# SBUF homes of a fused attention and feed-forward kernel: all operands of the 128x512 matmuls at one remainder modulo 512 bytes

## The chip, the cores and the metric

The kernel runs on one core of a Trainium2 chip. The metric is the time of one execution on the device in microseconds (us); a single execution of it is also recorded by the hardware profiler, which gives a start and an end for nearly every instruction. SBUF is the on-chip memory that the engines read their operands from; an address here is the byte offset of a tile within each of the 128 partitions.

## The reference

The inputs are q, k and v of shape (4, 8, 768, 64) in float32 and two weights in float64, `w_in` (512 x 2048) and `w_out` (2048 x 512). Attention is local (window of 16) with a summary key and value for each block of 32 positions, and its output is the input of a feed-forward layer:

```python
k_sum = k.reshape(B, H, nb, block, D).max(axis=3)
v_sum = v.reshape(B, H, nb, block, D).mean(axis=3)
scores_l = scale * np.matmul(q, k.transpose(0, 1, 3, 2))          # |i - j| < 16 is kept
scores_s = scale * np.einsum('bhsd,bhnd->bhsn', q, k_sum) + np.log(block)
a = softmax(concatenate([scores_l_masked, scores_s], axis=-1))
x = np.matmul(a, concatenate([v, v_sum], axis=2))                 # to (3072, 512)
h = x @ w_in
g = h * np.tanh(softplus(h))
return (g @ w_out).astype(np.float32)
```

## The kernel before

**The feed-forward part.** The 3072 tokens are worked in 6 groups `g` of 512, and the 2048 hidden units in 16 blocks `fc` of 128, so there are 96 steps `(g, fc)`. Every factor is held as two tiles, an upper and a lower part (`hi`/`lo`, `xh`/`xl`, `ah`/`al`), and each product is made of three matmuls. `ff_in` (L421) makes the hidden block `ph` with 12 matmuls (L427): four slices `cc` of `w_in` as the stationary operand, `xh` and `xl` as the moving one, 512 columns each. `ff_act` (L434) takes it out of PSUM, `ff_split` (L443, L445) makes `ah` and `al` of it. `ff_out` (L447) adds to four output tiles `po` with 12 matmuls (L455): four slices of `ah` or `al` are stationary, `w_out` moves, 512 columns each. One step is thus two groups of 12 matmuls of 128x512, a `ph` group and a `po` group, and there are 96 x 24 = 2304 such matmuls. In each group the three of a triple come in the order upper times upper, upper with the other's lower part, lower.

**Weights.** The weights arrive as 64-bit words and are split on ScalarE and VectorE into `hi` and `lo` during the first part of the run. Blocks `fc` 0 to 9 lie in the tiles `w_early_in`, `w_early_out`, blocks 10 to 15 in `w_late_in`, `w_late_out`. The late tiles take over the room of the pools `first_att` and `first_more` (L165, L166), which serve the first attention units and are closed at L587.

**Attention.** Each unit is a chunk of 256 positions and a pair of heads: scores `sc` (L317, for the first units L321 and L323), exponents and their sums on ScalarE and VectorE (L339, L350), normalizing on GpSimd (L370), four transposes `pt_ps` (L376), values `x_ps` (L397, L403), and the split into `xh` and `xl` (L413, L414). Units of the next token group stand between the `ph` and `po` groups of the present one.

**Order.** The order of the instructions is written out by hand: a list of short words (L546) for the first steps, where `ph`, `po` and the weight work are mixed, and after it a loop in which step `i` issues `ff_in` of step `i`, the attention work that falls due, and `ff_out` of step `i - 2` (L635). So in the loop `ph` and `po` groups alternate. Nothing reorders it (`tc.manual_schedule()`, L581).

**Homes.** A pool is opened on one of two sides of SBUF, and tiles get addresses in the order in which the pools are opened: `left` upwards, `right` downwards from the top. The pools are opened at L65 to L71.

Of the kernel before, what the change touches and what calls it, by code (L numbers as in the profile page):

```python
# [9 lines left out]
F32 = mybir.dt.float32  # L10
# [10 lines left out]
P = 128  # L21
# [18 lines left out]
EARLY = 10  # L40
# [17 lines left out]
def fused_kernel(ctx: ExitStack, tc: tile.TileContext, q0, qk, kt, v0, vw, vs, w_in, w_out, out):  # L58
# [3 lines left out]
    def pool(name, bufs, side):  # L62
        return ctx.enter_context(tc.tile_pool(name=name, bufs=bufs, side=side))

    const = pool("const", 1, "left")  # L65
    xp = pool("xp", 2, "left")
    w_out_home = pool("w_out_home", 1, "right")
    ff = pool("ff", 3, "right")
    stage = pool("stage", 2, "left")
    small = pool("small", 8, "right")  # L70
    att = pool("att", 2, "right")  # L71
    ps_o = ctx.enter_context(tc.tile_pool(name="ps_o", bufs=4, space=PS))

    ps_w = ctx.enter_context(tc.tile_pool(name="ps_w", bufs=4, space=PS))
# [27 lines left out]
    def weight_tiles(pools, name, blocks):  # L102
        return [[home.tile([P, blocks, WP], F32R, name=f"{name}_{w}_{part}") for part in ("hi", "lo")]
                for w, home in zip(("in", "out"), pools)]

    early = weight_tiles((const, w_out_home), "w_early", EARLY)
    late = []

    def weight(w, part, fc):
# [460 lines left out]
    def parse(word):  # L570
        name = next(m for m in sorted(ops, key=len, reverse=True) if word.startswith(m))
        return name, word[len(name):]
# [10 lines left out]
    for k, word in enumerate(order):  # L583
        name, what = parse(word)
# [101 lines left out]
```

## Time and profile before

| | |
|---|---|
| runs | 642.46, 643.26, 644.35 us (median 643.26) |
| the profiled execution | 643.47 us, of which the span from the first to the last instruction is 641.8 us |
| busy: TensorE matmul / weight load | 625.0 us / 510.3 us |
| busy: VectorE / ScalarE / GpSimd | 288.8 us / 270.3 us / 74.8 us |
| TensorE clock granted, mean over the span | 0.997 of full speed |

How to read it: the ends of matmuls in the trace are modelled and overlap the next matmul, so the mean duration of a matmul is not its cost. What a matmul costs is the time from its start to the start of the next one, called its *pitch* below. The timeline gives starts to 0.01 us; the pitch of one matmul is therefore read over several.

### The profile page before, as it was taken

Reading aid. Unit: us, or ns where it says so; the run is one execution under the profiler, and the core shown is the slowest. Engines: PE = TensorE matmul, PEld = TensorE weight load, DVE = VectorE, ACT = ScalarE, POOL = GpSimd, SP = SyncE. Lnnn points to the kernel's source line nnn. Section 1 sums busy time; section 2 is a strip of 40 time slices with the busy share of each in tenths; the row PEclk is TensorE's granted clock in tenths of the full one; section 3 lists DMA queues with packets and bytes.
Section 4 is the critical chain, followed back from the end, with each engine's and each line's share of the span. In section 5 each row is a group of like instructions: output and inputs, shape, how many; then the busy total and the mean of one; then the engine's idle time right before and its main releaser. Section 6 shows DMA issues by size and latency. Waiting matters only on the chain.

```text
span 641.8 us, 10991 instructions
## 1 busy us (share of the span) xinstructions
PE 625.0 (97%) x4272; PEld 510.3 (80%) x4272; DVE 288.8 (45%) x817; ACT 270.3 (42%) x659; POOL 74.8 (12%) x119
## 2 busy tenths in 40 slices
PE   4899899999999999999999999999999999999997
PEld 4787788777888888888888888888888888888885
DVE  4999999984232435323223445423232232222221
ACT  4986668582433425414425434245244251111111
POOL 4421131120101001001001011010010010000000
PEclk9999899999999999999999999999999999999999
DMA  9977765642212234603203254333133010100001
GB/s 285 280 243 261 229 228 191 209 161 96 64 46 76 84 112 115 215 1 96 83 14 95 91 150 131 90 91 95 66 95 86 11 32 1 65 1 0 1 0 66
DMA packets 31780, 68.24 MB, mean 106 GB/s; under 512 B 6768, under 2 KB 11632, under 8 KB 31728
## 3 DMA queue, kind: packets, MB, share of 16 engines
q1 hardware_dynamic: 31728, 67.53, 33.7%
q8 instruction: 34, 0.56, 0.4%
q14 instruction: 18, 0.15, 0.1%
HBM read 59.11 MB, written 6.29 MB: 102 GB/s over the span
## 4 chain that ended last, share of the span: by engine, by line
PE 90%; DVE 5%; DMA 1%; issue 1%; ACT 1%; POOL 1%; SPq 0%; POOLq 0%
PE po L455 41%; PE ph L427 39%; PE x_ps L403 3%; PE pt_ps L376 3%; PE sc L317 3%; DVE pr L339 1%; DMA q<-q 1%; DVE w_f L153 1%; DMA vw<-vm 1%; POOL pr L370 1%; DVE w L140 1%; PE sc L321 0%; DVE w_f L148 0%; DVE km L244 0%; DVE w L144 0%
## 5 line engine op out<-in xcount | busy, mean ns | idle before, releaser
L434 ACT ACTIVATE a<-ph 128x512 f32<-128x512 f32 x96 | 57.3, 598 | 249.1 <-PE ph L427 165.5
L443 DVE CAST ah<-a 128x512 fp32r<-128x512 f32 x80 | 34.1, 426 | 237.3 <-ACT a L434 235.9
L370 POOL TENSOR_TENSOR pr<-pr,rs 128x480 f32<-128x480 f32 x48 | 54.9, 1144 | 360.7 <-DVE rs L366 211.3
L455 PE MATMUL po<-w_early_out_hi,ah 128*128 128x512 f32 x240 | 96.0, 400 | 0.0
L427 PE MATMUL ph<-xh,w_early_in_hi 128*128 128x512 f32 x240 | 95.3, 397 | 0.0
L455 PE MATMUL po<-w_early_out_hi,al 128*128 128x512 f32 x240 | 94.5, 394 | 0.1
L427 PE MATMUL ph<-xh,w_early_in_lo 128*128 128x512 f32 x240 | 94.2, 392 | 0.0
L455 PE MATMUL po<-w_early_out_lo,ah 128*128 128x512 f32 x240 | 94.0, 392 | 0.0
L427 PE MATMUL ph<-xl,w_early_in_hi 128*128 128x512 f32 x240 | 93.4, 389 | 0.0
L350 ACT ACTIVATE pr<-pr,nm 128x120 f32<-128x120 f32 x192 | 73.3, 384 | 8.9 <-DVE nm L339 8.7
L445 DVE TENSOR_TENSOR al<-a,ah 128x512 fp32r<-128x512 f32 x96 | 68.7, 716 | 3.4 <-ACT ah L443 0.7
L455 PE MATMUL po<-w_late_out_hi,ah 128*128 128x512 f32 x144 | 57.5, 400 | 0.0
L427 PE MATMUL ph<-xh,w_late_in_hi 128*128 128x512 f32 x144 | 57.5, 399 | 0.0
L455 PE MATMUL po<-w_late_out_hi,al 128*128 128x512 f32 x144 | 56.8, 395 | 0.0
L455 PE MATMUL po<-w_late_out_lo,ah 128*128 128x512 f32 x144 | 56.7, 394 | 0.0
L427 PE MATMUL ph<-xh,w_late_in_lo 128*128 128x512 f32 x144 | 56.6, 393 | 0.0
L427 PE MATMUL ph<-xl,w_late_in_hi 128*128 128x512 f32 x144 | 56.1, 389 | 0.0
L455 PEld LDWEIGHTS po<-w_early_out_hi,ah 128*128 128x128 f32 x240 | 45.5, 189 | 11.3 <-issue 1.9
L427 PEld LDWEIGHTS ph<-xh,w_early_in_lo 128*128 128x128 f32 x240 | 45.0, 188 | 10.5
L455 PEld LDWEIGHTS po<-w_early_out_lo,ah 128*128 128x128 f32 x240 | 45.4, 189 | 9.8
L455 PEld LDWEIGHTS po<-w_early_out_hi,al 128*128 128x128 f32 x240 | 45.5, 190 | 9.6 <-DVE al L445 0.6
L427 PEld LDWEIGHTS ph<-xl,w_early_in_hi 128*128 128x128 f32 x240 | 45.2, 188 | 9.7
(77 smaller groups left out, 825.4 us busy)
## 6 DMA issues: line engine op xcount, KB each, us to landing
qk<-qk SPq DMA_DIRECT2D x40, 496.0 KB
w<-w_in SPq DMA_DIRECT2D x16, 512.0 KB
w<-w_out SPq DMA_DIRECT2D x16, 512.0 KB
vw<-vw SPq DMA_DIRECT2D x40, 192.0 KB
ks<-kt SPq DMA_DIRECT2D x16, 384.0 KB
out<-o SPq DMA_DIRECT2D x24, 256.0 KB
vsum<-vs SPq DMA_DIRECT2D x12, 384.0 KB
vw<-vm SPq DMA_DIRECT2D x40, 48.0 KB
```

The source lines that it names most:

```text
L140: nc.vector.tensor_scalar(out=x, in0=x, scalar1=29, scalar2=None, op0=ALU.logical_shift_right)
L153: nc.vector.scalar_tensor_tensor(out=u, in0=u, scalar=3, in1=words(k)[0], op0=ALU.logical_shift_left, op1=ALU.bitwise_or)
L317: nc.tensor.matmul(ps[h][row, at0:at0 + KA], u["qk"][r, s, h * QT:(h + 1) * QT], u["qk"][r, s, P:], start=True, stop=True)
L350: nc.scalar.activation(pr[:, s, :], pr[:, s, :], AF.Exp, scale=-1.0, bias=nm[:, s:s + 1], accum_out=sm[:, s:s + 1])
L370: nc.gpsimd.tensor_mul(u["p"], u["p"], u["r"].unsqueeze(2).broadcast_to([P, NQ, KA]))
L376: nc.tensor.transpose(ps[:KA, s * P:(s + 1) * P], u["p"][:, s, :], ident)
L403: nc.tensor.matmul(x, u["v"][0:rows, s, d], pt, start=(c >= CG), stop=(c >= CG or s == NQ - 1))
L427: nc.tensor.matmul(ph, w[:, cc * P:(cc + 1) * P], x[:, cc, :], start=(cc == 0 and n == 0), stop=(cc == NCC - 1 and n == 2))
L434: nc.scalar.activation(a, st[g, fc], AF.Mish)
L443: (nc.scalar.copy if g == 0 else nc.vector.tensor_copy)(ah, a)
L445: return lambda: nc.vector.tensor_sub(al, a, ah.bitcast(F32))
L455: nc.tensor.matmul(po[g][t], a[:, tok], w, start=(fc == 0 and n == 0), stop=(fc == NFC - 1 and n == 2))
```

## The change

Only the homes change. The pools `small` and `att` move from the right side to the left, ahead of the weights; a gap of 64 bytes (16 floats) is put behind them; the early `w_in` tiles get a pool of their own; and pools are opened in another order. Both programs, built, have the same instructions in the same order on every engine, with the same semaphore waits; only addresses in SBUF differ.

```diff
     const = pool("const", 1, "left")
+    small = pool("small", 8, "left")
+    att = pool("att", 2, "left")
+    aligned = pool("aligned", 1, "left")
+    w_in_home = pool("w_in_home", 1, "left")
+    w_out_home = pool("w_out_home", 1, "right")
     xp = pool("xp", 2, "left")
-    w_out_home = pool("w_out_home", 1, "right")
     ff = pool("ff", 3, "right")
     stage = pool("stage", 2, "left")
-    small = pool("small", 8, "right")
-    att = pool("att", 2, "right")
...
-    early = weight_tiles((const, w_out_home), "w_early", EARLY)
+    aligned.tile([P, 16], F32, name="gap")
+    early = weight_tiles((w_in_home, w_out_home), "w_early", EARLY)
```

The addresses of the built programs, with the remainder modulo 512 bytes in brackets. Every slice that a 128x512 matmul reads begins a whole number of 512 bytes into its tile, so a tile has one remainder for all its slices.

| tile | role | before | after |
|---|---|---|---|
| `w_early_in` hi | stationary of `ph`, fc 0 to 9 | 3104 (32) | 24544 (480) |
| `w_late_in` hi | stationary of `ph`, fc 10 to 15 | 97312 (32) | 118752 (480) |
| `xh`, first | moving of `ph` | 44064 (32) | 65504 (480) |
| `ah`, first | stationary of `po` | 176096 (480) | 176096 (480) |
| `w_early_out` hi | moving of `po`, fc 0 to 9 | 188384 (480) | 188384 (480) |
| `w_late_out` hi | moving of `po`, fc 10 to 15 | 121952 (96) | 143328 (480) |
| `vw`, loop units | stationary of `x_ps` | 160736 (480) | 18080 (160) |
| `pt`, loop units | moving of `x_ps` | 167904 (480) | 167904 (480) |
| `qk`, first | both operands of `sc` | 148960 (480) | 6304 (160) |

The `lo` tiles, `xl` and `al` have the remainders of their upper parts, before and after. All shifts are whole multiples of 64 bytes.

## Rows read from the trace of the kernel before

**Rows 1.** The page, part 1: busy us (share of the span), number of instructions.
```profile
PE 625.0 (97%) x4272; PEld 510.3 (80%) x4272; DVE 288.8 (45%) x817; ACT 270.3 (42%) x659; POOL 74.8 (12%) x119
```

**Rows 2.** The chain of work that ended last, 200 us to the end, shares by line.
```profile
by line: PE po L455 46.2%; PE ph L427 44.0%; PE x_ps L403 3.4%; PE sc L317 2.9%; PE pt_ps L376 2.8%; DVE o L466 0.2%; issue 0.0%
```

**Rows 3.** All waits of TensorE: who waited for whom, total us, times, longest.
```profile
PE sc L321 <- DMA q<-q: 7.3, 1, 7.3
PE pt_ps L376 <- POOL pr L370: 2.6, 2, 1.7
PE x_ps L403 <- DMA vw<-vm: 1.8, 1, 1.8
PE x_ps L397 <- ACT vm L261: 0.9, 1, 0.9
```

**Rows 4.** Three stretches: length, busy us (instructions) by engine, TensorE clock, DMA share, GB/s.
```profile
71.00:75.00 4.00, 4.00 (x14) 3.19 (x13) 4.00 (x12) 1.39 (x3) 0.00 (x0) 0.59 0.45 143
75.00:200.00 125.00, 125.00 (x785) 100.47 (x784) 83.59 (x185) 72.96 (x157) 18.59 (x20) 1.00 0.46 149
200.00:300.00 100.00, 100.00 (x671) 81.84 (x670) 39.19 (x130) 40.22 (x102) 8.99 (x16) 1.00 0.34 100
```

**Rows 5.** Groups of instructions, the page, part 5: two of TensorE's (xcount | busy, mean ns).
```profile
L455 PE MATMUL po<-w_early_out_hi,ah 128*128 128x512 f32 x240 | 96.0, 400 | 0.0
...
L455 PE MATMUL po<-w_late_out_hi,ah 128*128 128x512 f32 x144 | 57.5, 400 | 0.0
```

**Rows 6.** Timeline of TensorE (start, us): three `ph` groups and the next start.
```profile
47.05 0.39 PE L427 MATMUL ph<-xh,w_early_in_hi 128*128 128x512 f32 x1
...
49.77 0.39 PE L427 MATMUL ph<-xh,w_early_in_hi 128*128 128x512 f32 x1
...
55.21 0.39 PE L455 MATMUL po<-w_early_out_hi,ah 128*128 128x512 f32 x1
```

**Rows 7.** Timeline of TensorE: group starts in five alternating pairs, early weights.
```profile
566.04 0.39 PE L427 MATMUL ph<-xh,w_early_in_hi 128*128 128x512 f32 x1
...
568.80 0.39 PE L455 MATMUL po<-w_early_out_hi,ah 128*128 128x512 f32 x1
...
571.53 0.39 PE L427 MATMUL ph<-xh,w_early_in_hi 128*128 128x512 f32 x1
...
593.50 0.39 PE L427 MATMUL ph<-xh,w_early_in_hi 128*128 128x512 f32 x1
```

**Rows 8.** Timeline of TensorE: group starts in two alternating pairs, late weights.
```profile
615.53 0.40 PE L427 MATMUL ph<-xh,w_late_in_hi 128*128 128x512 f32 x1
...
618.29 0.39 PE L455 MATMUL po<-w_late_out_hi,ah 128*128 128x512 f32 x1
...
621.07 0.40 PE L427 MATMUL ph<-xh,w_late_in_hi 128*128 128x512 f32 x1
...
626.61 0.40 PE L427 MATMUL ph<-xh,w_late_in_hi 128*128 128x512 f32 x1
```

**Rows 9.** Timeline of TensorE: second matmul and next group's start, after attention work, twice.
```profile
305.14 0.39 PE L427 MATMUL ph<-xl,w_late_in_hi 128*128 128x512 f32 x1
...
307.66 0.39 PE L455 MATMUL po<-w_early_out_hi,ah 128*128 128x512 f32 x1
...
315.64 0.40 PE L455 MATMUL po<-w_early_out_hi,al 128*128 128x512 f32 x1
...
318.16 0.39 PE L427 MATMUL ph<-xh,w_late_in_hi 128*128 128x512 f32 x1
```

**Rows 10.** Groups of TensorE's instructions, 44 to 641 us: values of attention (xcount | busy us, mean ns).
```profile
L403 PE MATMUL x_ps<-pt,vw 120*64 120x64 f32 x618 | 23.2, 226 | 1.8 <-DMA vw<-vm 1.8
```

**Rows 11.** Timeline of TensorE: the last wait, and matmuls at the lower clock behind it.
```profile
69.95 0.69 PE L403 MATMUL x_ps<-pt,vw 120*64 120x64 f32 x16 [1.78 <-DMA vw<-vm]
...
71.66 0.63 PE L455 MATMUL po<-w_early_out_hi,al 128*128 128x512 f32 x1
...
72.08 0.63 PE L455 MATMUL po<-w_early_out_lo,ah 128*128 128x512 f32 x1
```

## The prediction

> **What bounds the kernel now.** I read the page's busy times first, then the chain of work that ended last, then the waits, and last the timeline of TensorE start by start. TensorE is busy for 97% of the span [rows 1]. From 200 us on, the chain is TensorE and little else: 46.2% of it is `po`, 44.0% `ph`, 9.1% attention [rows 2]. TensorE's waits that the trace shows are five in number and 12.6 us in all, and the last of them is the 1.8 us for `vw` [rows 3], which ends at 69.95 us [rows 11]. Behind it TensorE is never idle, while VectorE is busy for 83.6 us of 125 and later 39.2 of 100, ScalarE for 73.0 and 40.2 [rows 4]. So from about 71 us on the kernel takes as long as the sum of TensorE's pitches, and a shorter pitch shortens the run directly, with much cover left on the other engines. I count on no gain ahead of 71 us.
>
> Most of that sum is 2304 matmuls of 128x512, in 96 pairs of a `ph` and a `po` group: 240 + 144 in each of six kinds [rows 5], so 60 pairs are of early blocks and 36 of late ones. The mean durations in [rows 5] are the same, 400 ns, for early and late, but they overlap; the pitch is what tells.
>
> **Three pitches, and the remainders that go with them.** Three `ph` groups in a row, 36 matmuls, take 55.21 - 47.05 = 8.16 us: 226.7 ns each, and each group of 12 takes 2.72 us, the first matmuls included [rows 6]. Here every operand lies at remainder 32. I call this pitch settled. Where `ph` and `po` alternate with early blocks, remainder 32 in one group and 480 in the other, a `ph` group takes 2.76 us and a `po` group 2.73 [rows 7]: more than 2.72, although inside each group all remainders are equal. Over five pairs it is 27.46 / 5 = 5.492 us, against 24 x 0.2267 = 5.440 settled: 0.052 us too much. With late blocks, where the stationary `ah` is at 480 and the moving `w_out` at 96, the `po` group takes 2.78 us and the pair 11.08 / 2 = 5.540: 0.100 us too much [rows 8]. So I read it like this: the weight load of the next matmul runs while the present one streams; where both begin at the same remainder the pitch settles at 226.7 ns; a change of remainder between groups disturbs it for some matmuls; and a lasting difference (384 bytes in late `po`) never lets it settle. The row that speaks most for the address and not the start of a group is [rows 6]: two group starts without a change of remainder, no loss at either. Why the hardware does this no row shows; only the pairing of pitch and remainder is seen.
>
> The Trainium skill speaks against this change. "TensorE: Matmul & The Clock Gate", Part 2 (What happens when you issue a matmul), says that TensorE has two independent SBUF read ports, and that loading the next weights takes no read bandwidth from the running matmul; by that, addresses would not matter and the change would be worth nothing. The trace does not agree on its face: 2.78 against 2.73 us for two `po` groups of the same shapes [rows 7, 8]. The chance of that reading stands under the rivals as C.
>
> **The change part by part.** No instruction and no wait is added, removed or moved; the semaphore values are the same. So the sum has these terms only.
>
> 1. *Before, loss against the settled pitch.* 60 pairs x 0.052 + 36 x 0.100 = 3.1 + 3.6 = 6.7 us, if every pair alternated. In the hand-ordered first part some groups follow one of their own kind, as in [rows 6], and have no loss to give: about 12 group starts at half a pair's early loss, 0.026 us, are 0.3 us. That leaves 6.4.
> 2. *After, loss that stays.* Where attention matmuls stand between two groups, the pitch has to settle anew whatever the addresses. The timeline has 43 such returns. Two of them: from the second matmul to the next group's start, 11 pitches, 2.52 us after transposes and 2.52 after scores [rows 9], against 11 x 0.2267 = 2.493: 0.027 us each, 43 x 0.027 = 1.2 us. The starts are given to 0.01 us, so one return may be 0.02 to 0.06, which is 0.9 to 2.6 us. The first matmul of a return, which also carries the end of the attention work, I leave as it is. I take 1.4 us, near the two rows and a little above, because a long disturbance now runs on into the next group.
> 3. *Gain:* 6.4 - 1.4 = 5.0 us, bounds 3.8 and 5.5. Ahead of 71 us about 0.1 of it would be lost in the wait for `vw`; that is within the bounds.
> 4. *Attention matmuls.* `sc` has both operands in one tile, whose difference does not change. The transposes' slices begin 480 bytes after one another, so they have several remainders before and after. `x_ps` alone turns from equal remainders (480, 480) to unequal ones (160, 480): busy for 23.2 us from 44 us on [rows 10]. No row shows `x_ps` at unequal remainders. The nearest is late `po` against the settled pitch, 2.78 / 2.72, 2%: 0.5 us of 23.2. As those are matmuls of another shape, I take 0.2 us lost, and keep 0.5 lost and 0.5 gained as ends.
> 5. *VectorE, ScalarE, GpSimd, DMA.* Their tiles move by whole multiples of 64 bytes. I take nothing for this: a per cent more on VectorE would be 0.8 us of the 41 it has free between 75 and 200 us [rows 4].
>
> The sum: 643.47 of the profiled execution - 5.0 + 0.2 = 638.7. The profiled execution is 0.2 us above the median of the runs, so as a median I give **638.6 us**, 0.7% less than before.
>
> **The rivals.**
>
> *A, forecast:* all groups settle, 638.6. With the ends of terms 3 and 4 it lies between 643.47 - 5.5 - 0.5 = 637.5 and 643.47 - 3.8 + 0.5 = 640.2.
>
> *B, half of it:* only one of the two disturbances goes. If only the late `po` groups settle, 36 x (2.78 - 2.73) = 1.8 us, 641.5. If only the changes between groups go, and late `po` stays as it is for a reason that is not its remainder (its place between other pools, say), about 5.0 - 1.8 = 3.2, 640.3. For it speaks that the two are told apart in the trace by one tile pair alone.
>
> *C, no effect:* the loss at alternation comes from what alternates besides the address (the accumulator that is written, the waits at a group's start), and late `po` from something that stays: 643.3. [rows 6] speak against it for `ph` after `ph`; no row here shows a `ph` group followed by `po` at equal remainder.
>
> *D, slower:* with `ph` and `po` all at one remainder, the unsettled course that late `po` has becomes everyone's, because equal addresses make the two reads collide more, and not less, once nothing shifts them. The price: 2304 x (2.78 / 12 - 0.2267) = 11.5 us above settled, where 6.4 stand now: 643.5 + 5.1 = 648.6. It makes the kernel slower from the point at which more than about half of the groups take that course. Against it: equal remainders are settled at 32 [rows 6], and `po` at 480 comes down to 2.73 a group [rows 7].
>
> A smaller matter beside these: behind the wait for `vw` the granted clock is 0.59 of full speed in the mean over 4 us [rows 4], and a matmul then has a pitch of 0.42 us, the 1.2 GHz level, not 0.23 [rows 11]. If the gap of 1.8 us falls otherwise, some 7 matmuls gain or lose 0.2 us each, 1.4 us either way. It widens the range at both ends a little.
>
> **How the numbers follow.** A 0.72, B 0.11, C 0.11, D 0.06. A measurement of this kernel can tell 0.3% from no change, 1.9 us, so faster means below 641.3 and slower above 645.2. Faster: A and nearly all of B's upper form, 0.80. Same: C and B's weaker form, 0.14. Slower: D, 0.06. The range holds A with its bounds and the clock's part, and B up to the edge: 637.0 to 641.5.
>
> **What would show it.** In the timeline after the change, groups of 12 should take 2.72 us from start to start wherever no attention work stands ahead of them, `ph` and `po`, early and late alike: an early pair 5.44, a late pair 5.44. Late `po` at 2.78 would be B or D; early pairs still at 5.49, C or B. The busy time of `x_ps` should stay within half a microsecond of 23.2. The waits of TensorE should be the four lines of before, none behind 71 us; a new one there would mean that the gain was handed to another engine. What would make me wrong in the first place is that remainder modulo 512 bytes is not the quantity that matters, but something that goes along with it in these few tiles.

## The result

The changed kernel took 637.56, 637.59, 637.91 and 638.55 us: median 637.75, against 643.81 for the four runs of the kernel before beside it. The ratio is 0.991, with a 95% interval of 0.989 to 0.993. In a second comparison six runs had a median of 639.64 against 643.80 of 23 runs: 0.993, interval 0.991 to 0.996. So it is faster by 0.7 to 0.9%, and the forecast was 638.6.

The profiled execution took 637.56 us, its span 635.9 us instead of 641.8. The lines moved down by three: `ph` is L430 and `po` L458 now, `x_ps` L406.

The group starts that answer to [rows 7] and [rows 8], from the timeline of TensorE of the changed kernel (start, duration with a modelled end):

```profile
562.46 0.39 PE L430 MATMUL ph<-xh,w_early_in_hi 128*128 128x512 f32 x1
...
565.18 0.39 PE L458 MATMUL po<-w_early_out_hi,ah 128*128 128x512 f32 x1
...
567.90 0.39 PE L430 MATMUL ph<-xh,w_early_in_hi 128*128 128x512 f32 x1
...
610.06 0.39 PE L430 MATMUL ph<-xh,w_late_in_hi 128*128 128x512 f32 x1
...
612.78 0.39 PE L458 MATMUL po<-w_late_out_hi,ah 128*128 128x512 f32 x1
...
615.50 0.39 PE L430 MATMUL ph<-xh,w_late_in_hi 128*128 128x512 f32 x1
...
620.94 0.39 PE L430 MATMUL ph<-xh,w_late_in_hi 128*128 128x512 f32 x1
```

Every group of 12 takes 2.72 us here, `ph` and `po`, early and late: 226.7 ns a matmul. Before it was 2.76 and 2.73 with early weights and 2.76 and 2.78 with late ones [rows 7, 8]. After attention work the pitch still has to settle, as in [rows 9]:

```profile
302.85 0.40 PE L430 MATMUL ph<-xl,w_late_in_hi 128*128 128x512 f32 x1
...
305.36 0.39 PE L458 MATMUL po<-w_early_out_hi,ah 128*128 128x512 f32 x1
...
313.29 0.39 PE L458 MATMUL po<-w_early_out_hi,al 128*128 128x512 f32 x1
...
315.81 0.39 PE L430 MATMUL ph<-xh,w_late_in_hi 128*128 128x512 f32 x1
```

From the second matmul on, eleven pitches take 2.51 and 2.52 us against 2.493 settled, so 0.02 and 0.03 us too much.

**Where the 5.9 us of the span went.** Groups can be counted through in both traces. The 51st of the 192 begins just behind 200 us, and from there on the work is the same loop. Its start, in the kernel before and then in the changed one:

```profile
204.09 0.47 PE L427 MATMUL ph<-xh,w_late_in_hi 128*128 128x512 f32 x1
```

```profile
202.75 0.48 PE L430 MATMUL ph<-xh,w_late_in_hi 128*128 128x512 f32 x1
```

From there to the end of the span it is 641.8 - 204.1 = 437.7 us before and 635.9 - 202.8 = 433.1 after: 4.6 us gained. In the two profiles of the changed kernel this stretch agrees to 0.1 us, which the first 200 us do not: in the second one the first `ph` group began at 47.8 us instead of 44.3, and the stretch from group 51 on was again 433.1 us long. Of the kernel before there is one profile. So the experiments below are compared by this stretch.

The other 1.3 us lie ahead of group 51, and most of them are not the pitch. Stretches (length, busy us and number of instructions by engine, clock, DMA share, GB/s) that answer to [rows 4]:

```profile
71.00:75.00 4.00, 4.00 (x20) 3.30 (x19) 4.00 (x12) 1.35 (x3) 0.00 (x0) 1.00 0.45 155
75.00:200.00 125.00, 124.27 (x784) 100.03 (x783) 83.03 (x185) 73.39 (x158) 18.70 (x20) 1.00 0.45 149
200.00:300.00 100.00, 100.00 (x675) 82.58 (x674) 39.71 (x131) 40.28 (x103) 9.69 (x16) 1.00 0.33 100
```

Between 71 and 75 us the granted clock was 1.00 instead of 0.59. The starts of the ninth and the tenth group, before and then after:

```profile
71.08 0.78 PE L455 MATMUL po<-w_early_out_hi,ah 128*128 128x512 f32 x1
...
75.41 0.39 PE L455 MATMUL po<-w_early_out_hi,ah 128*128 128x512 f32 x1
```

```profile
70.88 0.48 PE L458 MATMUL po<-w_early_out_hi,ah 128*128 128x512 f32 x1
...
73.72 0.39 PE L458 MATMUL po<-w_early_out_hi,ah 128*128 128x512 f32 x1
```

The ninth group took 4.3 us before, with matmuls at the 1.2 GHz level [rows 11], and 2.8 after, which is 1.5 us. TensorE's wait a little ahead of it was 1.6 us instead of 1.8. In the second profile of the changed kernel this group took 2.85 us; of the experiments' kernels below, `alt_kept`, with the homes of before, has it at 2.85, and `all_32`, with those of after, at 4.43. So either time is seen with either layout, and I count the 1.5 us as a matter of how the start falls out, not as a gain of the addresses; with one or two profiles of a kernel that is not shown. Between 75 and 200 us TensorE is no longer busy throughout: 124.27 of 125. All its waits, as in [rows 3]:

```profile
PE sc L324 <- DMA q<-q: 8.1, 2, 7.3
PE x_ps L406 <- ACT a L437: 1.6, 1, 1.6
PE pt_ps L379 <- POOL pr L373: 1.2, 1, 1.2
PE po L458 <- DVE al L448: 0.4, 1, 0.4
PE sc L320 <- POOL qk L283: 0.4, 1, 0.4
PE ph L430 <- DVE w_late_in_lo L164: 0.3, 1, 0.3
```

The fourth and the last are new, stand behind 71 us, and are waits for VectorE (the fifth, new as well, is at 12 us, ahead of the first group). In the timeline the two stand at 101 and 121 us, in the changed kernel:

```profile
100.94 0.47 PE L458 MATMUL po<-w_early_out_hi,ah 128*128 128x512 f32 x1
101.81 0.50 PE L458 MATMUL po<-w_early_out_hi,al 128*128 128x512 f32 x1 [0.40 <-DVE al L448]
...
120.38 0.39 PE L430 MATMUL ph<-xl,w_late_in_hi 128*128 128x512 f32 x1
121.10 0.50 PE L430 MATMUL ph<-xh,w_late_in_lo 128*128 128x512 f32 x1 [0.33 <-DVE w_late_in_lo L164]
```

The pitches there are 0.87 and 0.72 us; at the same two matmuls before it was 0.32 and 0.37. That is 0.9 us given back. The `al` that the first of them waits for, on VectorE, before and then after:

```profile
101.02 0.68 DVE L445 TENSOR_TENSOR al<-a,ah 128x512 fp32r<-128x512 f32 x1
```

```profile
101.07 0.69 DVE L448 TENSOR_TENSOR al<-a,ah 128x512 fp32r<-128x512 f32 x1
```

VectorE was no earlier with it, and TensorE came to it 1.8 us earlier (that group began at 100.94 us instead of 102.71), 1.5 us of that from the clock. The chain of work that ended last says the same for 75 to 200 us, first of the kernel before, then of the changed one:

```profile
by line: PE po L455 45.7%; PE ph L427 43.9%; PE x_ps L403 4.3%; PE pt_ps L376 3.1%; PE sc L317 3.1%
```

```profile
by line: PE ph L430 30.6%; PE po L458 25.6%; DVE w L147 4.4%; issue 4.2%; DVE al L448 3.8%; DVE w L143 3.3%; DVE w_f L156 2.9%; PE x_ps L406 2.8%; DVE w_f L151 2.5%; PE sc L320 2.4%; ACT pr L353 2.2%; DVE w_early_out_lo L164 1.9%; DVE vq L2
```

It was TensorE alone, and up to 121 us it now runs through the weight work on VectorE. (The view breaks off where the last line does.) From the start of the tenth group to that of the 51st it took 128.7 us before and 129.0 after: the two groups with the new waits took 1.0 us more, all others together 0.6 less. So the 5.9 us of the span are 0.2 up to the ninth group, 1.5 of the clock, 0.4 lost from there to group 51, and 4.6 behind it.

### The profile page after: what moved, and what is told of

Same layout as the page of the kernel before. It is cut to its first block, busy times and chain, and to the rows that moved or that the text cites. A ratio compares the mean times of both kernels' runs of the same rounds, so it can differ in the third digit from the quotient of the medians.

```text
span 635.9 us, 10991 instructions
## 1 busy us (share of the span) xinstructions
PE 620.0 (98%) x4272; PEld 510.2 (80%) x4272; DVE 288.3 (45%) x817; ACT 270.2 (42%) x659; POOL 74.7 (12%) x119
## 4 chain that ended last, share of the span: by engine, by line
PE 80%; DVE 6%; ACT 1%; issue 1%; DVEq 0%
PE po L458 37%; PE ph L430 36%; PE x_ps L406 3%; PE sc L320 2%; PE pt_ps L379 2%; DVE w L147 1%; DVE al L448 1%; DVE w L143 1%; DVE w_f L151 1%; DVE w_f L156 1%; DVE w_early_out_lo L164 1%; ACT pr L353 0%; DVE vq L268 0%; DVE km L247 0%; DVE pr L342 0%
## 5 line engine op out<-in xcount | busy, mean ns | idle before, releaser
L446 DVE CAST ah<-a 128x512 fp32r<-128x512 f32 x80 | 34.5, 432 | 233.5 <-ACT a L437 232.1
L458 PE MATMUL po<-w_early_out_hi,ah 128*128 128x512 f32 x240 | 95.2, 397 | 0.0
L430 PE MATMUL ph<-xh,w_early_in_hi 128*128 128x512 f32 x240 | 94.4, 393 | 0.0
L458 PE MATMUL po<-w_early_out_hi,al 128*128 128x512 f32 x240 | 93.8, 391 | 0.5 <-DVE al L448 0.4
L458 PE MATMUL po<-w_early_out_lo,ah 128*128 128x512 f32 x240 | 93.6, 390 | 0.0
L430 PE MATMUL ph<-xh,w_early_in_lo 128*128 128x512 f32 x240 | 93.4, 389 | 0.0
L430 PE MATMUL ph<-xl,w_early_in_hi 128*128 128x512 f32 x240 | 93.4, 389 | 0.0
L458 PE MATMUL po<-w_late_out_hi,ah 128*128 128x512 f32 x144 | 57.0, 396 | 0.0
L430 PE MATMUL ph<-xh,w_late_in_hi 128*128 128x512 f32 x144 | 56.8, 395 | 0.0
L430 PE MATMUL ph<-xh,w_late_in_lo 128*128 128x512 f32 x144 | 56.2, 390 | 0.3 <-DVE w_late_in_lo L164 0.3
L458 PE MATMUL po<-w_late_out_lo,ah 128*128 128x512 f32 x144 | 56.1, 390 | 0.0
L458 PE MATMUL po<-w_late_out_hi,al 128*128 128x512 f32 x144 | 56.1, 390 | 0.0
L430 PE MATMUL ph<-xl,w_late_in_hi 128*128 128x512 f32 x144 | 56.1, 389 | 0.0
L458 PEld LDWEIGHTS po<-w_early_out_hi,ah 128*128 128x128 f32 x240 | 45.0, 188 | 10.8 <-issue 1.9
L458 PEld LDWEIGHTS po<-w_early_out_hi,al 128*128 128x128 f32 x240 | 45.1, 188 | 10.2 <-DVE al L448 1.4
L458 PEld LDWEIGHTS po<-w_early_out_lo,ah 128*128 128x128 f32 x240 | 45.1, 188 | 9.5
L430 PEld LDWEIGHTS ph<-xh,w_early_in_lo 128*128 128x128 f32 x240 | 45.0, 188 | 9.4
L430 PEld LDWEIGHTS ph<-xl,w_early_in_hi 128*128 128x128 f32 x240 | 45.1, 188 | 9.0
```

What stands on the lines that cost most here:

```text
L430: nc.tensor.matmul(ph, w[:, cc * P:(cc + 1) * P], x[:, cc, :], start=(cc == 0 and n == 0), stop=(cc == NCC - 1 and n == 2))
L446: (nc.scalar.copy if g == 0 else nc.vector.tensor_copy)(ah, a)
L458: nc.tensor.matmul(po[g][t], a[:, tok], w, start=(fc == 0 and n == 0), stop=(fc == NFC - 1 and n == 2))
```

## The experiments

Theory T: the pitch depends on the difference between the address that the running matmul streams from and the address of the next weight load; at difference zero it settles at 226.7 ns. The rivals are the ones of the prediction, B (one disturbance only, or the place of a tile), C (something else that alternates) and D. All kernels below but the first need some free SBUF for gaps; they take it from a scratch area at the bottom of SBUF (`dynamic_dma_scratch_size`, 1024 to 256 bytes; this line is left out of the edits shown). So the left side begins 768 bytes lower, and the gaps allow for it. A gap is a tile that nothing uses, in floats of 4 bytes. The kernels have the instructions, the order and the waits of the changed kernel, and differ in addresses alone.

**The changed kernel again** (`after_again`).

> The changed kernel again, to stand beside the three partial ones on one chip. Every theory: about 6 us below the kernel before (637.8 against 643.8).

639.64 us, given above; group 51 to the end 433.1 us. Its runs spread from 637.39 to 641.45, so a difference of 2 us between kernels can't be read from whole runs safely, and the stretch is what tells.

**Late `po` alone back at remainder 96** (`late_back`), near the place that it has in the changed kernel; the first gap keeps `w_in` at 480.

```diff
-    aligned = pool("aligned", 1, "left")
+    pool("gap0", 1, "left").tile([P, 80], F32, name="gap0")
...
+    pool("gap4", 1, "right").tile([P, 96], F32, name="gap4")
...
-    aligned.tile([P, 16], F32, name="gap")
```

> All operands stay at remainder 480 except w_late_out, which goes back to 96, at nearly the same place in SBUF. Theory T (the pitch settles when the running matmul's moving operand and the next stationary operand have equal remainders): late po groups take 2.78 us again, the ph groups behind them about 2.76, early pairs stay at 5.44; the loss is about 36 x (0.06 + 0.03) = 3 us, so about 641. Rival P (late po was slow by its place in SBUF, not by its remainder): no difference to the changed kernel, 637.8.

640.22 us, 0.995 of before (0.994 to 0.997). Group 51 to the end is 435.5 us, so 2.4 of the 4.6 us are lost again. Group starts in its timeline, a late pair and the next, behind an early group:

```profile
610.36 0.39 PE L430 MATMUL ph<-xh,w_late_in_hi 128*128 128x512 f32 x1
...
613.08 0.40 PE L458 MATMUL po<-w_late_out_hi,ah 128*128 128x512 f32 x1
...
615.87 0.39 PE L430 MATMUL ph<-xh,w_late_in_hi 128*128 128x512 f32 x1
...
618.61 0.40 PE L458 MATMUL po<-w_late_out_hi,ah 128*128 128x512 f32 x1
...
621.40 0.39 PE L430 MATMUL ph<-xh,w_late_in_hi 128*128 128x512 f32 x1
```

Late `po` takes 2.79 us, the `ph` ahead of the first of them 2.72, the one between them 2.74. The tile moved by 384 bytes and keeps its neighbours, so its place is not the cause, its remainder is. The after-effect in `ph` was expected at 0.03 to 0.04 us; behind the last attention work it is 0.015 us in five of the six `ph` groups that follow a late `po`, and 0.05 in one.

**Only late `po` mended** (`alt_kept`): the kernel before with `w_late_out` at 480, while `ph` stays at 32 (the first gap) and the rest of `po` at 480.

```diff
+    pool("gap0", 1, "left").tile([P, 64], F32, name="gap0")
     const = pool("const", 1, "left")
...
     att = pool("att", 2, "right")
+    pool("gap4", 1, "right").tile([P, 32], F32, name="gap4")
```

> The kernel before with w_late_out alone brought to 480: po is at 480 throughout and ph at 32, as before. Theory T: late po takes 2.73 us instead of 2.78, early pairs 5.49 as before, late pairs 5.49; the gain on the kernel before is about 36 x 0.05 = 1.8 us, so 0.3%. Rival Q (the whole gain of the change came from late po, the alternation costs nothing by itself): about 6 us faster than before, as the changed kernel. Rival P: no difference to the kernel before.

642.07 us, 0.998 of before (0.997 to 0.999); group 51 to the end 436.2 us, 1.5 less than before and 3.1 more than after. In its timeline the late pairs have become early ones:

```profile
608.31 0.39 PE L429 MATMUL ph<-xh,w_late_in_hi 128*128 128x512 f32 x1
...
611.08 0.39 PE L457 MATMUL po<-w_late_out_hi,ah 128*128 128x512 f32 x1
...
613.81 0.39 PE L429 MATMUL ph<-xh,w_late_in_hi 128*128 128x512 f32 x1
```

2.77 and 2.73 by these starts (2.76 and 2.73 in the mean of the late groups), where [rows 8] have 2.76 and 2.78. So the alternation costs by itself, and Q falls. Both disturbances are real; B is out in either form.

**All at remainder 32** (`all_32`): one gap ahead of `w_in`, one at the top of the right side.

```diff
-    aligned = pool("aligned", 1, "left")
+    pool("gap0", 1, "left").tile([P, 96], F32, name="gap0")
     w_in_home = pool("w_in_home", 1, "left")
+    pool("gap5", 1, "right").tile([P, 112], F32, name="gap5")
...
-    aligned.tile([P, 16], F32, name="gap")
```

> All operands of the 128x512 matmuls at remainder 32 instead of 480. Theory T (only the difference counts): the same as the changed kernel within 0.1%, all groups 2.72 us. Rival R (480 is a good place by itself, 32 a bad one): ph and po groups at 2.76 us, about 4 us slower than the changed kernel.

638.75 us, 0.993 of before (0.991 to 0.995). Group 51 to the end is 433.4 us, and behind the last attention work every group takes 2.72 us. So 32 is as good as 480, and R falls.

This run also shows where the two waits for VectorE come from. Its ninth group took 4.43 us (granted clock 0.66 between 73 and 78 us), about as long as before. Here `al` and the first two matmuls of the group that had to wait:

```profile
103.00 0.68 DVE L448 TENSOR_TENSOR al<-a,ah 128x512 fp32r<-128x512 f32 x1
```

```profile
105.05 0.48 PE L458 MATMUL po<-w_early_out_hi,ah 128*128 128x512 f32 x1
105.36 0.40 PE L458 MATMUL po<-w_early_out_hi,al 128*128 128x512 f32 x1
```

`al` is there before TensorE is, the two pitches are 0.31 and 0.50 us instead of 0.87 and 0.72, and from the tenth group to the 51st the time is 128.2 us, 0.5 less than before. From the start of the ninth group to the end it is 566.0 us against 570.7 before: 4.7 us gained where the clock falls alike.

**The scans** (`scan1` to `scan4`). Four gaps give each kind of group a constant difference of its own between stationary and moving operand. The edit of the first, which sets early `ph` to -64 (`gap1`), early `po` to -192 (`gap3`), late `ph` to +128 (`gap2`) and late `po` to +192 (`gap4`); the sizes differ in the others:

```diff
-    aligned = pool("aligned", 1, "left")
+    pool("gap0", 1, "left").tile([P, 64], F32, name="gap0")
     w_in_home = pool("w_in_home", 1, "left")
+    pool("gap1", 1, "left").tile([P, 16], F32, name="gap1")
     w_out_home = pool("w_out_home", 1, "right")
     xp = pool("xp", 2, "left")
+    pool("gap3", 1, "right").tile([P, 48], F32, name="gap3")
     ff = pool("ff", 3, "right")
     stage = pool("stage", 2, "left")
+    pool("gap2", 1, "left").tile([P, 32], F32, name="gap2")
+    pool("gap4", 1, "right").tile([P, 48], F32, name="gap4")
...
-    aligned.tile([P, 16], F32, name="gap")
```

> Constant differences d = (next stationary operand) - (running moving operand), modulo 512, one for each kind of group: ph early -64, ph late +128, po early -192, po late +192; the remainders also change between groups. Theory T (a difference disturbs, and only zero settles): every kind has a mean pitch above 228 ns in the matmuls 6 to 11 of a group, that of the +384 = -128 of late po before (232.9) being typical; about 233 on all 2304 would be 12 us over settled, some 650 in all. Theory S (a small shift is as good or better, as single matmuls at a change of 64 had 226): -64 at 227 or below. Theory M (the period is shorter than 512 bytes, 64 or 128): these settle at 226.7 like zero.

> As the first scan: ph early -256, ph late +64, po early -128, po late +256. Theory T: all above 228 ns, po early -128 about 232.9 as late po at the same difference before, and ph -256 equal to po +256, since they are the same modulo 512. Theory M with a period of 256: the two 256s at 226.7. Theory S: +64 at 227 or below.

> As the first scan, small ones: ph early -32, ph late +32, po early -96, po late +96. Theory T in its strict form: all above 228 ns. In a softer form, small differences settle a little off 226.7, and there is a width in bytes inside which the pitch is as good as settled: -32 and +32 between 225 and 228, the 96s near 230. Theory M with a period of 32: -32, +32 and the 96s at 226.7.

> As the first scan, the differences left: ph early -160, ph late +160, po early -224, po late +224. Theory T: all above 228 ns. Theory S (one of the differences beats zero): one of the sixteen of the four scans lies below 226.

One run each: 646.83, 646.19, 651.77 and 652.56 us, beside 644.38 of the kernel before. From group 51 to the end it is 440.6, 439.7, 443.6 and 443.8 us, more than the 437.7 of before and the 433.1 of after. The first scan was expected at some 650 us, which took 233 ns on all 2304 matmuls for 12 us over settled; 2304 x 6.3 ns are 14.5. The four times lie on both sides of 650.

The time of a group, from its first start to the next group's, as a mean over the 6 to 10 groups of its kind behind the last attention work:

| difference, bytes | group, us | group with the opposite sign, us |
|---|---|---|
| 0 (changed kernel) | 2.720 | |
| -32 / +32 (`ph`) | 2.791 | 2.792 |
| -64 / +64 (`ph`) | 2.776 | 2.793 |
| -96 / +96 (`po`) | 2.807 | 2.809 |
| -128 (`po`) / +128 (`ph`) | 2.779 | 2.785 |
| -160 / +160 (`ph`) | 2.799 | 2.805 |
| -192 / +192 (`po`) | 2.793 | 2.750 |
| -224 / +224 (`po`) | 2.800 | 2.796 |
| -256 (`ph`) / +256 (`po`) | 2.753 | 2.747 |

Read modulo 256, pairs that should be equal nearly are: -192 and +64 take 2.793 both, -96 and +160 2.807 and 2.805, -128 and +128 2.779 and 2.785; -64 and +192 are the widest apart, 2.776 and 2.750. These times hold the disturbance at the change of group too, since the kinds have different differences. Where groups of one kind follow one another it is gone. Three `ph` groups in a row, as in [rows 6], first at -64 (`scan1`), then at -256 (`scan2`):

```profile
47.71 0.39 PE L433 MATMUL ph<-xh,w_early_in_hi 128*128 128x512 f32 x1
...
50.46 0.39 PE L433 MATMUL ph<-xh,w_early_in_hi 128*128 128x512 f32 x1
...
53.21 0.39 PE L433 MATMUL ph<-xh,w_early_in_hi 128*128 128x512 f32 x1
...
55.95 0.39 PE L461 MATMUL po<-w_early_out_hi,ah 128*128 128x512 f32 x1
```

```profile
48.28 0.39 PE L433 MATMUL ph<-xh,w_early_in_hi 128*128 128x512 f32 x1
...
51.00 0.39 PE L433 MATMUL ph<-xh,w_early_in_hi 128*128 128x512 f32 x1
...
53.72 0.39 PE L433 MATMUL ph<-xh,w_early_in_hi 128*128 128x512 f32 x1
...
56.44 0.39 PE L461 MATMUL po<-w_early_out_hi,ah 128*128 128x512 f32 x1
```

At -64 a group takes 2.747 us for good: (55.95 - 47.71) / 3. The same three groups take 2.80 us each at -32 (`scan3`) and 2.81 at -160 (`scan4`). At -256 it is 2.72, the settled time. `po` at +256 takes that as well, in the last groups of the program (`scan2`):

```profile
634.97 0.39 PE L461 MATMUL po<-w_late_out_hi,ah 128*128 128x512 f32 x1
...
637.69 0.39 PE L461 MATMUL po<-w_late_out_hi,ah 128*128 128x512 f32 x1
```

So 256 bytes are as good as none. S falls (no difference settles below 226.7 ns; at +64 matmuls 6 to 11 have a mean of 233.4), and so does M in its short forms (32, 64 and 128 do not settle); with a period of 256 it holds. T's softer form falls as well: at -32 and +32 these matmuls have 233.5 and 233.1 ns, not 225 to 228. For `po` at -128 T had forecast 232.9, and it is 232.8. T in the form "512" was too strict.

**Two remainders that lie 256 apart** (`two_256`), to test that in the whole kernel: `w_in`, `xh` and `w_late_out` at 224, `ah`, `al` and `w_early_out` at 480.

```diff
-    aligned = pool("aligned", 1, "left")
+    pool("gap0", 1, "left").tile([P, 16], F32, name="gap0")
...
+    pool("gap4", 1, "right").tile([P, 64], F32, name="gap4")
...
-    aligned.tile([P, 16], F32, name="gap")
```

> Two remainders that lie 256 bytes apart: all of ph at 224, ah and al and w_early_out at 480, w_late_out at 224. So ph and po alternate between remainders, and late po reads its two operands 256 bytes apart. Theory T256 (the scans' 256 settled like zero: only the difference modulo 256 counts): every group 2.72 us, from group 50 to the end 433.1 us as in the changed kernel, some 638 to 640 in all. Strict T with 512: disturbances as in the kernel before at each change of group, and late po not settled: group 50 to the end about 437, some 643.

638.48 us, 0.991 of before (0.987 to 0.995), and group 51 to the end 433.1 us: the changed kernel's own number (the expectation counts the groups from 0, so its 50 is 51 here). A late pair in its timeline, whose two groups have differences of 0 and +256:

```profile
610.53 0.39 PE L430 MATMUL ph<-xh,w_late_in_hi 128*128 128x512 f32 x1
...
613.25 0.39 PE L458 MATMUL po<-w_late_out_hi,ah 128*128 128x512 f32 x1
...
615.97 0.39 PE L430 MATMUL ph<-xh,w_late_in_hi 128*128 128x512 f32 x1
```

2.72 and 2.72, and no disturbance at the change from 224 to 480. Strict 512 is out.

## Why the prediction was right, point by point

- **The direction and the size** held: 638.6 forecast, medians of 637.75 and 639.64. (The prediction's own sum gives 638.5: 643.47 - 5.0 + 0.2, less the 0.2 by which the profiled execution lies above the median. Nothing hangs on it.) A was the case that came; B, C and D were refuted by `late_back` with `alt_kept`, by the settled alternation of the changed kernel, and by its time. The tell-tale that the prediction named, 2.72 us for every group without attention work ahead, is there to the digit: from the 51st on, in all 86 groups that have none ahead and none right behind.
- **Terms 1 to 3** named a loss of 6.4 us before, 1.4 after, and so a gain of 5.0, bounds 3.8 and 5.5. Added up pitch by pitch from the tenth group on (without group 25, which waits, and without the first matmuls of returns, as in the prediction), the loss against 226.7 ns went from 6.2 to 1.2 us; from group 51 on alone, from 5.1 to 0.5. So the terms were right one by one. Most returns lose what those of [rows 9] lose; a few, all ahead of group 51, lose 0.04 to 0.06 us.
- **Where the gain lies** was wrong in part. I had TensorE's pitches set the time from 71 us on, with cover left on VectorE, and by term 5 nothing to fear from it. Between the tenth and the 51st group two new waits for VectorE took 1.0 us, more than the 0.6 that the pitch gave there. It is the sign that the prediction named, a new wait behind 71 us. The step that failed read a mean: VectorE busy for 83.6 of 125 us [rows 4] says nothing on the two or three places where its result is wanted next. In the kernel before one of those pitches was already 0.37 us instead of 0.23, and not listed among its waits.
- **The clock** was luck. The prediction allowed 1.4 us either way for the slow matmuls behind 70 us; in this execution it was 1.5 us to the good. It also brought TensorE to the two waits that much earlier, so about 0.9 of it went to VectorE. With hardly any of either, as in `all_32`, 4.7 us are gained from the ninth group on; the 5.9 of this span is not the measure of the addresses.
- **Term 4**, `x_ps` at unequal remainders, is nil:

```profile
L406 PE MATMUL x_ps<-pt,vw 120*64 120x64 f32 x622 | 23.3, 226 | 1.6 <-ACT a L437 1.6
```

  The mean duration is 226 ns as in [rows 10]. (The four more are an effect of where 44 us falls; the whole trace has 768 on this line, 28.8 us busy, before and after.) What counts is again the pitch: from 200 us on, the matmuls of `x_ps` follow one another every 30.0 ns in all eleven traces, with differences between `vw` and `pt` of 0, 32, 64, 128, 160 and 192 bytes modulo 256. The 0.2 us taken for the term were not there; these small matmuls do not answer to the remainder as the 128x512 ones do.
- **The quantity** was half right. The prediction's last sentence named as the risk that the remainder modulo 512 only goes along with what matters. It did: by the scans and `two_256`, 256 is the period, and before there was no tile pair 256 apart to tell the two from each other.
- **The page of the Trainium skill** that was set against the change ("TensorE: Matmul & The Clock Gate", Part 2) has the weight load take nothing from the running matmul's reads. What the prediction drew from it, that addresses would not matter, does not hold for this stream: with instructions, order and waits untouched, a group took 2.72 us or up to 2.81, by the address alone. The measurement decides. Whether it is the read that is held up, no run shows.

Open stays what in the chip does it. That two reads meet in the same part of SBUF at some differences is a picture that would fit a period of 256 bytes, but no row shows a port or a bank, and none of the runs could. Open is also which pair counts. The two operands of one matmul alone cannot be it, since with early blocks before they are equal throughout and the change of group still costs; T's pair, running moving operand and next weight load, covers both the change and the lasting difference. But within a group the two pairs have the same difference, and no run tells T from two causes side by side.

## What to carry to other kernels

Where TensorE is the bound and each large matmul has its own weight load, read the pitch from start to start, not the mean duration: a few ns in 227 show up only there. Then look at the addresses: all stationary and moving tiles of neighbouring matmuls at one remainder modulo 256 bytes gave 226.7 ns here, a lasting mismatch up to 234, and even a change of remainder (by 64 bytes) between two well-matched groups cost 0.01 to 0.04 us each time. And ask of each stretch apart whether another engine takes over when the bound one gets faster; a busy share of two thirds was enough for that.

## What the runs showed of the hardware that was not expected

- The pitch repeats closely: between two profiles of the changed kernel, 433 us of work from group 51 on agreed to 0.1 us, while the start differed by 3.5 us, and in the kernel before, the ten early `po` groups behind the last attention work all take 2.73 us.
- In these scans the period is 256 bytes. Differences of 32, 96, 160 and 224 bytes give groups of 2.79 to 2.81 us, 128 gives 2.78; +192 and -64, equal modulo 256, come down to 2.75 (-64 where groups of its kind follow one another); 0 and 256 to 2.72. None is below.
- A lasting mismatch costs up to 3% of a group's time (2.81 against 2.72), and with the same instructions the kernel takes 652.56 us (`scan4`, one run) instead of 637.75.
